# One square per step in the output product, two accumulators apart, and a hinted last branch, in a fused attention and MLP kernel

## The chip, the cores and the metric

The kernel runs on one core of a Trainium2 chip. The metric is the time of one execution on the device, in microseconds (us); lower is better. The names of the engines in the profile are PE (TensorE matmul), PEld (the loading of its weights), DVE (VectorE), ACT (ScalarE), POOL (GpSimd) and SP (SyncE, which issues most transfers). A q behind a name (SPq, ACTq) marks an instruction that the engine's sequencer handles by itself.

## The reference

Attention with a few global columns and a local window over 2 x 768 tokens, 8 heads of 64, is followed by two MLPs on all 1536 tokens.

```python
attn = softmax(scores + bias, masked) @ v            # 2 x 768 tokens, 8 heads of 64
x  = attn.reshape(1536, 512)
xn = x / sqrt(mean(x * x) + 1e-6) * rms_g
g, val = xn @ w_gate, xn @ w_val                     # 512 x 1536 each
y  = (g * sigmoid(g) * val) @ w_out                  # p = g * sigmoid(g) * val; 1536 x 512
h  = relu(y @ w_in)                                  # 512 x 2048
out = (s * h * h + b) @ w_out2                       # 2048 x 512
```

## The kernel before

Weights arrive as float64 words; integer operations on DVE take them apart, and ACT and DVE make of each a high and a low float16 part. Activations are split in the same way, so that each product is three matmuls (`mm3`, L204 to L206: high x high, high x low, low x high). A matmul here is 128 x 128 x 512.

The program for the usual case (`fast_program`) is laid out by hand: each engine works through its own list in order, and waits where an operand isn't ready. After attention, `run` has four products in a row: gate and value (L543), output (L570), in (L622) and the last one (L664). Tokens stand in three blocks of 512 (b = 0, 1, 2).

In the **output product** a step (b, f) has 12 matmuls, three for each m of four accumulators. Ahead of step n+1, `split1(n + 1)` makes the two halves of p: `phi` on ACT (L537) and `plo` on DVE (L538, which reads `phi`). In a step L204 needs `phi`, L205 needs `plo`, and L206 needs `phi` again. The halves have two buffers. `tick` then lets the conversion of a weight advance: L305 and L330 on ACT, L310 to L321 and L335 on DVE.

A float16 program is only right where no value leaves float16's range, so statistics are kept. `see` takes one finished tile of p from the list `unseen` and squares it on ACT with a running sum (`peak`, L511, tile `junk`, and the reading of the sum). In the loop over gate and value one tile is seen after each (f, b); those left over are seen at L568, ahead of the first step of the output product. Near the end `verdict` reduces the statistics to one word, `ok_i`.

In the **last product** block 2 is worked in two passes, over the row tiles t = 0, 1 and t = 2, 3. Its four accumulators are halves of two tiles with two PSUM banks each (`ps("xx")`, t = 0, 1, and `ps("yy")`, t = 2, 3), while block 1 has four tiles of one bank (`ps("gv")`). After the last matmul `evac2` empties t = 2 on DVE (L661) and t = 3 in two halves, one on ACT (L653) and one on DVE (L654), and SP and ACT issue the transfers to `out` (L662, L656, L655).

Then each engine loads `ok_i` (L1218) and branches (L1219): where the word is zero, a general program computes everything again; else the branch leads past it to the end. The bounds given to `values_load` become a check of the word (FUSED_REGOPS and SEQ_ASSERT at L1218), which SP works off behind the second `If`.

Of the kernel before, what the change touches and what calls it, by code (L numbers as in the profile page):

```python
# [29 lines left out]
NB = B * S // BLK  # L30
# [32 lines left out]
def kernel(  # L63
# [17 lines left out]
    nc = tc.nc  # L81
# [70 lines left out]
    ok_i = cst.tile([1, 1], I32, name="ok_i")  # L152
# [9 lines left out]
    def ps(kind):  # L162
        m = banks[kind][turn[kind] % len(banks[kind])]
        turn[kind] += 1
        return psum[0].tile([128, 512] if m < 8 else [128, 2, 512], F32, name=f"ps{m}", tag=f"b{m}")

    def accumulators(second):
        if second:
            return [ps("gv") for _ in range(4)]
        return [t[:, j, :] for t in (ps("xx"), ps("yy")) for j in range(2)]  # L170
# [32 lines left out]
    def mm3(o, ahi, alo, bhi, blo, first, last):  # L203
        T.matmul(out=o, lhsT=ahi, rhs=bhi, start=first, stop=False)  # L204
        T.matmul(out=o, lhsT=ahi, rhs=blo, start=False, stop=False)  # L205
        T.matmul(out=o, lhsT=alo, rhs=bhi, start=False, stop=last)  # L206


    class Mlp:
# [313 lines left out]
        def run(self, done):  # L523
# [9 lines left out]
            def split1(n):  # L533
                b, f = order1[n]
                pt = self.pt.pop((f, b))
                phi, plo = parts[n] = self.split_tiles()
                A.activation(phi, pt, AF.Copy, scale=self.p_scale())  # L537
                V.scalar_tensor_tensor(  # L538
                    plo, in0=pt, scalar=self.p_scale(), in1=self.raw_of(phi), op0=ALU.mult, op1=ALU.subtract
                )  # L540
# [17 lines left out]
            def evac1(acc, yy, m):  # L558
                yhi, ylo = yy
                half = 0.5 * self.up("y") / self.up("p", "w")  # L560
                A.activation(yhi[:, m, :], acc[m], AF.Copy, scale=half)
                V.scalar_tensor_tensor(
                    ylo[:, m, :], in0=acc[m], scalar=half, in1=self.raw_of(yhi[:, m, :]), op0=ALU.mult, op1=ALU.subtract
                )

            self.flush()
            squares = []
            while self.unseen:  # L568
                self.see()
            for n, (b, f) in enumerate(order1):  # L570
                if f == 0:
                    acc = accumulators(b % 2)
                hi, lo = self.get("o", f)
                phi, plo = parts.pop(n)
                for m in range(4):
                    ms = slice(m * 128, (m + 1) * 128)
                    mm3(acc[m], hi[:, ms], lo[:, ms], phi, plo, f == 0, f == F1 - 1)
                if b == NB - 1:
                    self.drop("o", f)
                if n + 1 < len(order1):  # L580
                    split1(n + 1)
                if f == F1 - 1:
                    y[b] = self.new_xy()
                    for m in range(4):
                        self.later(1 + m, lambda acc=acc, b=b, m=m: evac1(acc, y[b], m))
                        squares.append((b, m))
                self.tick(2)
            self.flush()
            p1S.close()
            self.p0S.close()  # L590

# [15 lines left out]
            def split2(n):  # L607
                b, f, t0, t1 = order2[n]
                g = gt[(f, b)] if t1 < 4 else gt.pop((f, b))
                g = g[:, t0 * 128 : t1 * 128]  # L610
                phi, plo = parts[n] = [t[:, : (t1 - t0) * 128] for t in self.split_tiles()]
                A.activation(phi, g, AF.Identity, bias=b_col)  # L612
                V.scalar_tensor_tensor(plo, in0=g, scalar=b_col, in1=self.raw_of(phi), op0=ALU.add, op1=ALU.subtract)  # L613


            order2 = [(b, f, 0, 4) for fs in (range(F2 // 2), range(F2 // 2, F2)) for b in (0, 1) for f in fs]

            order2 += [(b, f, t0, t0 + 2) for b in range(2, NB) for t0 in (0, 2) for f in range(F2)]
            accs = {}
# [21 lines left out]
            with (  # L641
                tc.tile_pool(name="ow", bufs=F2 - RING) as ow,
                tc.tile_pool(name="ob", bufs=4, side="right") as ob,
            ):
                self.xpool["p"] = (ow, lambda f: f >= RING)

                down = 1.0 / self.up("g", "w")

                def evac2(acc, b, t):
                    o = ob.tile([128, BLK], F32, name="o", tag="o")  # L650
                    r0 = self.row_of[4 * b + t]
                    if (b, t) == (NB - 1, 3):
                        A.activation(o[:, HB:], acc[t][:, HB:], AF.Copy, scale=down)  # L653
                        V.tensor_scalar(o[:, :HB], acc[t][:, :HB], down, None, op0=ALU.mult)  # L654
                        nc.scalar.dma_start(out[r0 : r0 + 128, HB:], o[:, HB:])  # L655
                        nc.sync.dma_start(out[r0 : r0 + 128, :HB], o[:, :HB])  # L656
                        return
                    if t % 2:
                        A.activation(o, acc[t], AF.Copy, scale=down)
                    else:  # L660
                        V.tensor_scalar(o, acc[t], down, None, op0=ALU.mult)  # L661
                    nc.sync.dma_start(out[r0 : r0 + 128, :], o)  # L662

                for n, (b, f, t0, t1) in enumerate(order2):  # L664
                    if f == t0 == 0:
                        accs[b] = accumulators(b % 2)
                    acc = accs[b]
                    hi, lo = self.get("p", f)
                    phi, plo = parts.pop(n)
                    for t in range(t0, t1):  # L670
                        ts = slice((t - t0) * 128, (t - t0 + 1) * 128)
                        mm3(acc[t], phi[:, ts], plo[:, ts], hi, lo, f == 0, f == F2 - 1)
                    if n + 1 < len(order2):
                        split2(n + 1)
                    if self.half and n == len(order2) - 24:
                        self.verdict()
                    if f == F2 - 1:
                        for t in range(t0, t1):
                            self.later(1 + (t - t0) // 2, lambda acc=acc, b=b, t=t: evac2(acc, b, t))
                    self.tick(2)  # L680
                self.flush()
# [532 lines left out]
    rv = nc.values_load(fast_i[0:1, 0:1], min_val=0, max_val=1)  # L1214
    with tc.If(rv != 0):
        with tc.manual_schedule(), ExitStack() as fctx:
            fast_program(fctx)
    rv = nc.values_load(ok_i[0:1, 0:1], min_val=0, max_val=1)  # L1218
    with tc.If(rv == 0):  # L1219
        with ExitStack() as gctx:  # L1220
            general_program(gctx)

# [63 lines left out]
```

## Time and profile before

| | us |
|---|---|
| median of 3 runs | 649.4 (648.39 to 649.66) |
| profiled execution, its own time | 648.7 |
| profiled execution, span of the trace | 646.9 |
| PE busy in the span | 624.4 |
| DVE, ACT, POOL busy | 436.3, 310.4, 55.3 |

The span runs from the first to the last instruction on the core; the execution's own time has 1.8 us around it. Times within the trace are counted from the start of the span. Matmuls are pipelined: each is listed with 0.38 us, and in a full stream one starts some 0.22 us after the other.

### The profile page before, as it was taken

How to read it: one execution, taken by the hardware profiler on the slowest of the kernel's cores; microseconds unless marked ns; L12 is line 12 of the kernel's file. 1: busy time of each engine (PE TensorE's matmuls, PEld its weight loads, DVE VectorE, ACT ScalarE, POOL GpSimd, SP SyncE). 2: the span in 40 equal slices, each digit the busy share in tenths (PEclk: the TensorE clock that was granted, in tenths of full speed). 3: DMA queues.
4: the chain of work that ended last, by engine and by line, in shares of the span. 5: the costliest groups of instructions: out<-in, count | busy, mean ns of one | idle time of the engine just before them, and what ended most of it. 6: DMA issues, size and time to landing. Idle time of an engine off the chain costs nothing.

```text
span 646.9 us, 9387 instructions
## 1 busy us (share of the span) xinstructions
PE 624.4 (97%) x3379; PEld 318.8 (49%) x3379; DVE 436.3 (67%) x1103; ACT 310.4 (48%) x689; POOL 55.3 (9%) x59
## 2 busy tenths in 40 slices
PE   9889999999999999997999999999999999999994
PEld 6668777544444444443444444444444444444442
DVE  8898988435888768885342478888666788633452
ACT  4978868413444444465232346644333445333431
POOL 1445552300000000000000000000000000000000
PEclk9999999999999999998999999999999999999998
DMA  8673642001333323332100032333222232010001
GB/s 256 199 217 106 188 141 66 2 2 33 97 98 98 99 73 110 110 97 66 32 1 0 1 97 67 103 108 114 66 66 66 65 99 97 1 65 36 32 33 37
DMA packets 39419, 52.50 MB, mean 81 GB/s; under 512 B 4420, under 2 KB 31300, under 8 KB 39364
## 3 DMA queue, kind: packets, MB, share of 16 engines
q1 hardware_dynamic: 38690, 51.42, 25.4%
q8 instruction: 28, 0.46, 0.3%
q10 hardware_dynamic: 674, 0.39, 0.2%
q14 instruction: 27, 0.22, 0.1%
HBM read 48.66 MB, written 3.15 MB: 80 GB/s over the span
## 4 chain that ended last, share of the span: by engine, by line
PE 88%; DVE 5%; ACT 4%; issue 1%; POOL 1%; DVEq 0%; ACTq 0%; POOLq 0%
PE ps L204 27%; PE ps L206 26%; PE ps L205 26%; PE ps L991 2%; PE ps L972 2%; PE ps L920 2%; ACT t L948 1%; DVE t L933 1%; ACT junk L511 1%; ACT pt L979 1%; PE ps L428 1%; PE ps L441 1%; DVE xn L451 0%; PE ps L178 0%; DVE xyl L466 0%
## 5 line engine op out<-in xcount | busy, mean ns | idle before, releaser
L204 PE MATMUL ps<-hi_p,ev 128*128 128x512 f16 x192 | 72.8, 379 | 0.5 <-ACT ev L612 0.5
L206 PE MATMUL ps<-hi_p,ev 128*128 128x512 f16 x192 | 72.8, 379 | 0.3 <-DVE ev L613 0.3
L613 DVE SCALAR_TENSOR_TENSOR ev<-gt,sbs,ev 128x512 f16<-128x512 f32 (+1 forms) x64 | 39.5, 617 | 49.4 <-ACT ev L612 49.2
L204 PE MATMUL ps<-xyh,hi_i 128*128 128x512 f16 x192 | 72.8, 379 | 0.0
L205 PE MATMUL ps<-xyl,hi_i 128*128 128x512 f16 x192 | 72.8, 379 | 0.0
L206 PE MATMUL ps<-xyh,lo_i 128*128 128x512 f16 x192 | 72.8, 379 | 0.0
L205 PE MATMUL ps<-lo_p,ev 128*128 128x512 f16 x192 | 72.8, 379 | 0.0
L612 ACT ACTIVATE ev<-gt,sbs 128x512 f16<-128x512 f32 (+1 forms) x64 | 39.2, 614 | 66.0 <-PE ps L205 64.4
L204 PE MATMUL ps<-ev,hi_o 128*128 128x512 f16 x144 | 55.1, 382 | 4.7 <-ACT ev L537 4.7
L601 ACT ACTIVATE side<-ps 128x512 f32<-128x512 f32 x48 | 28.7, 597 | 64.2 <-PE ps L206 64.2
L538 DVE SCALAR_TENSOR_TENSOR ev<-p,ev 128x512 f16<-128x512 f32 x36 | 24.9, 692 | 50.1 <-ACT ev L537 50.1
L204 PE MATMUL ps<-xyh,hi_g 128*128 128x512 f16 (+1 forms) x160 | 57.3, 358 | 0.2 <-DVE p L1062 0.2
L204 PE MATMUL ps<-xyh,hi_v 128*128 128x512 f16 (+1 forms) x160 | 57.3, 358 | 0.1
L206 PE MATMUL ps<-xyh,lo_g 128*128 128x512 f16 (+1 forms) x160 | 57.2, 358 | 0.0
L206 PE MATMUL ps<-xyh,lo_v 128*128 128x512 f16 (+1 forms) x160 | 57.2, 358 | 0.0
L205 PE MATMUL ps<-xyl,hi_g 128*128 128x512 f16 (+1 forms) x160 | 57.2, 358 | 0.0
L205 PE MATMUL ps<-xyl,hi_v 128*128 128x512 f16 (+1 forms) x160 | 57.2, 358 | 0.0
L602 DVE SCALAR_TENSOR_TENSOR gt<-side,sbs 128x512 f32<-128x512 f32 x48 | 36.1, 752 | 29.1 <-ACT side L601 29.0
L205 PE MATMUL ps<-ev,hi_o 128*128 128x512 f16 x144 | 55.3, 384 | 0.4 <-DVE ev L538 0.4
L206 PE MATMUL ps<-ev,lo_o 128*128 128x512 f16 x144 | 55.3, 384 | 0.0
L537 ACT ACTIVATE ev<-p 128x512 f16<-128x512 f32 x36 | 22.6, 628 | 56.7 <-PE ps L206 56.7
L948 ACT ACTIVATE t<-t,mn 128x232 f32<-128x232 f32 (+1 forms) x96 | 44.2, 462 | 11.2 <-DVE mn L933 11.1
(152 smaller groups left out, 1080.0 us busy)
## 6 DMA issues: line engine op xcount, KB each, us to landing
raw_i<-in_moe_w_in_dram SPq DMA_DIRECT2D x16, 512.0 KB, 3.6
raw_p<-in_moe_w_out_dram SPq DMA_DIRECT2D x16, 512.0 KB, 3.5
raw_g<-in_moe_w_gate_dram SPq DMA_DIRECT2D x12, 512.0 KB, 3.8
raw_v<-in_moe_w_val_dram SPq DMA_DIRECT2D x12, 512.0 KB, 3.7
raw_o<-in_moe_w_out_dram SPq DMA_DIRECT2D x12, 512.0 KB, 3.5
vw<-in_v_dram SPq DMA_DIRECT2D x10, 512.0 KB, 3.8
q<-in_q_dram SPq DMA_DIRECT2D x11, 256.0 KB, 4.6
out_dram<-o SPq DMA_DIRECT2D x11, 256.0 KB, 2.1
```

Source lines behind the costliest of these rows:

```text
L204: T.matmul(out=o, lhsT=ahi, rhs=bhi, start=first, stop=False)
L205: T.matmul(out=o, lhsT=ahi, rhs=blo, start=False, stop=False)
L206: T.matmul(out=o, lhsT=alo, rhs=bhi, start=False, stop=last)
L537: A.activation(phi, pt, AF.Copy, scale=self.p_scale())
L538: V.scalar_tensor_tensor(plo, in0=pt, scalar=self.p_scale(), in1=self.raw_of(phi), op0=ALU.mult, op1=ALU.subtract)
L601: A.activation(r, o, AF.Relu, scale=1.0 / self.up("y", "w"))
L602: V.scalar_tensor_tensor(g, in0=r, scalar=s_col, in1=r, op0=ALU.mult, op1=ALU.mult, accum_out=self.stat["g"][:, n : n + 1] if self.half el ...
L612: A.activation(phi, g, AF.Identity, bias=b_col)
L613: V.scalar_tensor_tensor(plo, in0=g, scalar=b_col, in1=self.raw_of(phi), op0=ALU.add, op1=ALU.subtract)
L920: T.matmul(out=st["sc", g][:, j, pp, :], lhsT=st["q"][64 * j : 64 * j + 64, pr, :], rhs=st["k"][64 * j : 64 * j + 64, pr, :], start=True, ...
L948: A.activation(t[:, hh, :], t[:, hh, :], AF.Exp, bias=mn[:, hh : hh + 1], scale=-1.0, accum_out=sm[:, hh : hh + 1])
L972: T.transpose(tp[:, m, hh * 128 : (hh + 1) * 128], st["t", g][:, hh, m * kn : (m + 1) * kn], ident)
```

## The change

Four edits. The squares that were left over are no longer taken all at once ahead of the output product: `see` is called in each of its steps, behind `split1(n + 1)`. In the last product, the accumulators t = 2, 3 of block 2 are two `gv` tiles of one bank each. A place is marked at which a hint for the branch labelled "general" is asked for, and that `If` has the label. `values_load` of `ok_i` has no bounds.

```diff
             self.flush()
             squares = []
-            while self.unseen:
-                self.see()
             for n, (b, f) in enumerate(order1):
...
                 if n + 1 < len(order1):
                     split1(n + 1)
+                self.see()
                 if f == F1 - 1:
...
             self.flush()
+            assert not self.unseen
...
                     if f == t0 == 0:
                         accs[b] = accumulators(b % 2)
+                    if f == 0 and t0 == 2 and b == NB - 1:
+                        accs[b][2:] = [ps("gv") for _ in range(2)]
...
                     if self.half and n == len(order2) - 24:
                         self.verdict()
+                    if self.half and n == len(order2) - 2:
+                        tc.mark_branch_hint_location("general", "LikelyTaken")
...
-    rv = nc.values_load(ok_i[0:1, 0:1], min_val=0, max_val=1)
-    with tc.If(rv == 0):
+    rv = nc.values_load(ok_i[0:1, 0:1])
+    with tc.If(rv == 0, label="general"):
```

**ACT's list at the start of the output product.** `junk` is the square of a tile of p, `ev` is `phi`, and `u` and `hi_o` belong to the conversion of a weight. Before:

```order
L511 ACTIVATE junk,stat_p<-p 128x512 x9
L537 ACTIVATE ev_3122<-p 128x512
L305 ACTIVATE u<-raw_o 128x512
L537 ACTIVATE ev_3144<-p 128x512
L330 ACTIVATE hi_o<-u 128x512
L537 ACTIVATE ev_3166<-p 128x512
```

And in the changed kernel, from the same place:

```order
L511 ACTIVATE junk,stat_p<-p 128x512
L537 ACTIVATE ev_3114<-p 128x512
L511 ACTIVATE junk,stat_p<-p 128x512
L305 ACTIVATE u<-raw_o 128x512
L537 ACTIVATE ev_3137<-p 128x512
L511 ACTIVATE junk,stat_p<-p 128x512
L330 ACTIVATE hi_o<-u 128x512
L537 ACTIVATE ev_3160<-p 128x512
```

Nine squares stood ahead of the `phi` of step 1; now one does (the last that the loop over gate and value calls for), and the other eight stand one behind each of the next eight `phi`. DVE's list is the same in this stretch.

**DVE's list, and then ACT's, at the end of the last product** up to the branch on `ok_i`. The names carry their numbers here, and a row ends with what it waits for (PE, DVE, Activation and Pool are the engines, DMAHW the transfers). DVE before:

```order
L661 TENSOR_SCALAR o_5817<-ps9_5462 128x512 [waits DMAHW7_49,PE_49]
L654 TENSOR_SCALAR o_5820<-ps9_5462 128x256 [waits DMAHW4_49,DMAHW0_49,Activation_49]
L1215 UNCONDITIONAL_BRANCH
L1215 UNCONDITIONAL_BRANCH [waits DVE_49]
L1218 TENSOR_LOAD ok_i_107 [waits DVE_49,Pool_49]
```

DVE in the changed kernel:

```order
L661 TENSOR_SCALAR o_5819<-ps2_5647 128x512 [waits DMAHW7_49,PE_49]
L654 TENSOR_SCALAR o_5822<-ps3_5648 128x256 [waits DMAHW4_49,DMAHW0_49,Activation_49]
L1219 UNCONDITIONAL_BRANCH
L1219 UNCONDITIONAL_BRANCH [waits DVE_49]
L1222 TENSOR_LOAD ok_i_107 [waits DVE_49,Pool_49]
```

ACT before:

```order
L653 ACTIVATE o_5820<-ps9_5462 128x256 [waits DMAHW0_49,DVE_49]
L655 DMA out_0_dram<-o_5820 128x256 [waits Activation_49]
L1215 UNCONDITIONAL_BRANCH
L1215 UNCONDITIONAL_BRANCH [waits Activation_49]
L1218 TENSOR_LOAD ok_i_107 [waits DVE_49,Pool_49]
```

ACT in the changed kernel:

```order
L653 ACTIVATE o_5822<-ps3_5648 128x256 [waits DMAHW0_49,PE_49]
L655 DMA out_0_dram<-o_5822 128x256 [waits Activation_49]
L1219 UNCONDITIONAL_BRANCH
L1219 UNCONDITIONAL_BRANCH [waits Activation_49]
L1222 TENSOR_LOAD ok_i_107 [waits DVE_49,Pool_49]
```

L661 now reads another tile than L653 and L654 do, and L653 waits for PE where it waited for DVE; L654 still waits for ACT. No row for a hint stands ahead of the branch.

**The end of SP's list**, behind the transfers of the general program. Before:

```order
L282 DMA raw_o<-in_moe_w_out_dram 128x1024 x12
L276 DMA raw_i<-in_moe_w_in_dram 128x4x256 x16
L282 DMA raw_p<-in_moe_w_out_dram 128x1024 x16
L662 DMA out_dram<-o 128x512 x11
L656 DMA out_dram<-o 128x256
L1219 UNCONDITIONAL_BRANCH x2
L1218 ISA x2
L1281 UNCONDITIONAL_BRANCH
```

And in the changed kernel:

```order
L282 DMA raw_o<-in_moe_w_out_dram 128x1024 x12
L276 DMA raw_i<-in_moe_w_in_dram 128x4x256 x16
L282 DMA raw_p<-in_moe_w_out_dram 128x1024 x16
L662 DMA out_dram<-o 128x512 x11
L656 DMA out_dram<-o 128x256
L1223 UNCONDITIONAL_BRANCH x2
```

The two instructions of the check (ISA x2) and a branch behind them are gone. Apart from the moved squares and what is shown here, the lists of the usual program hold the same rows as before; none of an engine has a row for a hint.

## Rows read from the trace of the kernel before

**Rows 1.** The page, part 1: busy time, share of the span, instructions

```profile
PE 624.4 (97%) x3379; PEld 318.8 (49%) x3379; DVE 436.3 (67%) x1103; ACT 310.4 (48%) x689; POOL 55.3 (9%) x59
```

**Rows 2.** Waits: who waited for whom, us in total, times, longest

```profile
PE ps L204 <- ACT ev L537: 4.7, 1, 4.7
...
PE ps L204 <- ACT ev L612: 0.5, 1, 0.5
```

**Rows 3.** Timeline, start of the output product: start, duration, engine, line

```profile
288.00 0.61 ACT L511 ACTIVATE junk<-p 128x512 bf16<-128x512 f32 x1
...
288.74 0.63 ACT L511 ACTIVATE junk<-p 128x512 bf16<-128x512 f32 x1
...
289.76 0.69 DVE L318 SCALAR_TENSOR_TENSOR u<-raw_o,u 128x512 int32<-128x512 int32 x1
...
290.27 0.38 PE L206 MATMUL ps<-ev,lo_o 128*128 128x512 f16 x1
...
295.28 0.69 DVE L538 SCALAR_TENSOR_TENSOR ev<-p,ev 128x512 f16<-128x512 f32 x1 [4.83 <-ACT ev L537]
...
296.03 0.58 PE L205 MATMUL ps<-ev,hi_o 128*128 128x512 f16 x1 [0.35 <-DVE ev L538]
...
299.37 0.38 PE L204 MATMUL ps<-ev,hi_o 128*128 128x512 f16 x1
```

**Rows 4.** Windows: stretch, length, busy PE, PEld, DVE, ACT, POOL, PEclk, DMA

```profile
295.30:299.40 4.10, 3.75 (x10) 1.26 (x10) 4.07 (x8) 1.66 (x3) 0.00 (x0) 0.58 0.38 111
...
617.20:628.00 10.80, 10.29 (x49) 4.29 (x48) 5.43 (x26) 4.80 (x10) 0.00 (x0) 1.00 0.13 49
...
302.60:305.20 2.60, 2.60 (x14) 1.18 (x13) 1.93 (x6) 1.15 (x2) 0.00 (x0) 1.00 0.59 188
```

**Rows 5.** Timeline of two later steps of the output product

```profile
302.61 0.38 PE L204 MATMUL ps<-ev,hi_o 128*128 128x512 f16 x1
...
302.81 0.63 ACT L537 ACTIVATE ev<-p 128x512 f16<-128x512 f32 x1 [1.33 <-PE ps L206]
303.34 0.61 ACT L330 ACTIVATE hi_o<-u 128x512 f16<-128x512 f32 x1
...
304.08 0.69 DVE L335 SCALAR_TENSOR_TENSOR lo_o<-u,hi_o 128x512 f16<-128x512 f32 x1
...
305.14 0.69 DVE L318 SCALAR_TENSOR_TENSOR u<-raw_o,u 128x512 int32<-128x512 int32 x1
...
305.20 0.38 PE L204 MATMUL ps<-ev,hi_o 128*128 128x512 f16 x1
```

**Rows 6.** Timeline, end of the last product

```profile
637.37 0.38 PE L206 MATMUL ps<-hi_p,ev 128*128 128x512 f16 x1
...
638.01 0.38 PE L206 MATMUL ps<-hi_p,ev 128*128 128x512 f16 x1
638.43 0.69 DVE L661 TENSOR_SCALAR o<-ps 128x512 f32<-128x512 f32 x1 [1.78 <-PE ps L206]
...
639.16 0.38 ACT L653 ACTIVATE o<-ps 128x256 f32<-128x256 f32 x1 [3.02 <-DVE o L661]
...
639.57 0.42 DVE L654 TENSOR_SCALAR o<-ps 128x256 f32<-128x256 f32 x1 [0.45 <-ACT o L653]
640.02 0.33 SPq L656 DMA_DIRECT2D out_dram<-o  x1
```

**Rows 7.** Line 1219: count, ns min/median/max, first and last start us

```profile
L1219 SPq EVENT_SEMAPHORE  x8: 17/17/17, 644.7 to 645.2; - x8
...
L1219 SPq COMPARE_BRANCH  x1: 50/50/50, 641.3 to 641.3; - x1
```

**Rows 8.** Line 1218, the check on SP

```profile
L1218 SPq FUSED_REGOPS  x1: 164/164/164, 645.3 to 645.3; - x1
L1218 SPq SEQ_ASSERT  x1: 29/29/29, 645.5 to 645.5; - x1
```

**Rows 9.** Transfers: line, KB each, us from issue to landing

```profile
out_dram<-o SPq DMA_DIRECT2D x1, 128.0 KB, 2.1
```

## The prediction

> **What bounds the kernel now.** I read the page first: PE is busy for 624.4 of 646.9 us [rows 1], so time can only go where PE stands still, where its clock is low, or behind its last matmul. The waits tell where it stands still longest: once, 4.7 us, L204 for `phi` (ACT, L537) [rows 2]. The timeline puts this at step 1 of the output product [rows 3]: the last matmul of step 0 starts at 290.27, and ACT works off nine squares, the first at 288.00, one every 0.74 us, before it makes the `phi` that step 1 needs. PE takes up L205 at 296.03, and its starts come in their usual distance again only from 299.37. That distance is 0.216 us: twelve starts from 302.61 to 305.20 [rows 5]. [...] The second place is the end: from the last matmul at 638.01 to the end of the span, 8.9 us. There three evacuations run one behind the other, each waiting for the one before [rows 6], then the last transfer is issued, and SP passes its branch at 641.3 and goes on at 644.7 [rows 7].
>
> **The change part by part.** The sum is made against the profiled execution (648.7 us, span 646.9). The median of the three runs, 649.4, lies 0.7 above it, and I subtract the sum from the median.
>
> **Squares, what is removed.** From 290.27 to 299.37 ten matmuls start, which take 10 x 0.216 = 2.16 us in a full stream; 9.10 passed. So the pile of squares costs 6.94 us: some 5.3 of waiting, and 3.34 - 8 x 0.216 = 1.61 of low clock between 296.03 and 299.37 [rows 3].
>
> **Squares, what is left of the stall.** One square still stands ahead of the `phi` of step 1, so `phi` starts at 288.74, where the second square started, and ends before the step could start at 290.27 + 0.22 = 290.49: L204 doesn't wait. But `plo` (L538) stands behind L318 in DVE's list, which starts at 289.76 and takes 0.69; `plo` then starts at 290.45 at the latest. L205 came 0.75 after the start of `plo` (295.28 to 296.03), so it comes at 291.20 and not at 290.70: 0.50 us stay lost [rows 3]. The bounds are 0 (DVE starts instructions a little before the one ahead has ended) and 0.50 + 1.61 = 2.11, if the clock falls in spite of so short a wait. I take 0.50, since from 617.2 to 628 the clock stayed at 1.00 [rows 4] although PE stood still there for 0.5 us [rows 2]. The gain is 6.94 - 0.50 = 6.44, between 4.83 and 6.94.
>
> **Squares, where they go.** Eight of them now stand in steps 1 to 8, behind the `phi` of the next step, 0.74 us each. I cost them at nothing; the work that covers them is PE's, 2.59 us a step. ACT in a step: 0.53 from `phi` to the next start, 0.74 for the square, 0.61 for L330, or 1.88 [rows 5, 3]. What comes late is the weight conversion: L330 starts at 303.34 + 0.74 and ends 0.61 later, 304.69, so DVE's L335 starts 0.6 later than at 304.08, and with it L318, from 305.74 to 306.43 [rows 5]. Behind it in DVE's list is the `plo` of the step that starts at 305.20 + 2.59 = 307.79; it could start at 306.43 and let L205 go at 307.18, which is due at 308.0: 0.8 us to spare. The weight parts that are delayed are needed only some steps later. Were the cover gone, each square would cost up to 0.74, all eight 5.9.
>
> **Accumulators apart.** With t = 2 and t = 3 in tiles of their own, L661 waits only for the last matmul of t = 2. That one starts at 637.37, 0.64 before the last of all, and an evacuation starts 0.42 after such a start (638.01 to 638.43): L661 runs from 637.79 to 638.48, beside PE. L653 waits for PE instead of DVE, so it starts at 638.43 and not at 639.16. L654 still waits for L653: 0.41 later, at 638.84 instead of 639.57. The last transfer is issued 0.73 us earlier [rows 6]. Whether the end follows: the transfer lands 2.1 us after its issue [rows 9], at 642.1 as it is now, and SP comes to its waits at 644.7 [rows 7]; the landing is not what SP waits for, so everything behind moves with the issue. Gain 0.73, with 0 as the lower bound if another engine came last, and 1.07 as the upper, if L654 no longer stayed behind L653 (638.50 instead of 639.57).
>
> [...]
>
> **The check.** SP runs it between its waits and its end: 164 and 29 ns [rows 8]. SP's eight waits of 17 ns take 0.5 us [rows 7], so an instruction costs some 0.05 beyond its duration: 0.19 + 2 x 0.05 = 0.3 us, an estimate between 0.19 and 0.4. SP is alone there, and the end waits for it.
>
> **The hint.** The changed lists have no row for it on any engine, so I cost it at 0; the 3.3 us between SP's branch and its next instruction [rows 7] stay.
>
> **Sum:** 6.44 + 0.73 + 0.3 = 7.5 us. The profiled execution would take 641.2, the median 641.9.
>
> **The rivals.**
>
> *The hint works (chance 0.04).* If the branch did know its target ahead, SP would go on at 641.4 and wait for the landing at 642.1 in its sixth wait, which it now passes at about 645.05: 2.9 us less, 639.0. For it: DVE, ACT and SP each have a branch there, and SP's 3.3 us are a wait for nothing that the program computes. Against: the lists show nothing that would tell the sequencer. [...]
>
> *The clock still falls (0.08).* The wait that is left, 0.50 us or a little more, lets the clock fall as before: 1.61 us come back, 643.5. Against it is the stretch from 617.2.
>
> *The squares only move (0.04).* Each step waits for its square after all, 0.74 x 8 = 5.9 us: 647.8, faster by a quarter per cent. The spare 0.8 us would have to be wrong by as much.
>
> *Slower (0.03).* [...]
>
> *The squares move without cost and the stall stays (0.01).* Something else than the squares holds `phi` of step 1; no row names it. Then 648.4.
>
> **How the numbers follow.** My forecast, 7.5 us less, has 0.80. Its own range is from the bounds: 4.83 to 6.94, 0.19 to 0.4 and 0 to 1.07 are not all at one end together, so some 6.5 to 8.3, or 641.1 to 642.9. The three runs lie 1.0 below to 0.3 above their median, and the case with the low clock is at 643.5; the range 640.2 to 643.9 takes in both, and leaves out the working hint and the three dear cases, 0.12 with some noise beyond. A measurement of this kernel can tell about 0.2% (1.3 us) from no change. Faster by more: my forecast, the hint, the low clock, and half of the case in which the squares only move, 0.94; within 0.2%: 0.03; slower: 0.03.
>
> **What would show each step.** In the waits, L204 for `phi` of L537 goes from 4.7 us to nearly nothing and L205 for `plo` stays below 0.6; the clock has no stretch below 1.00 between 290 and 300; in the timeline one square stands in each step behind `phi`, and starts of PE in steps 1 to 8 come every 0.216 us. L653 starts with the last matmul's end and no longer after L661, and line 1222 has no FUSED_REGOPS on SP, while SP's branch is still followed by some 3.3 us. I would be wrong if PE waited for `plo` in each step, if the clock fell, if another engine came to the end later than SP, or if SP's gap had shrunk.

## The result and the profile after

| | before | after |
|---|---|---|
| median of 4 runs each, us | 648.89 (647.92 to 649.66) | 641.01 (640.72 to 643.17) |
| ratio, 95% interval | | 0.9886 (0.986 to 0.9913) |
| profiled execution: its time, its span | 648.7, 646.9 | 643.2, 641.4 |

By the medians the change makes the kernel 7.9 us faster, by the means of the four runs 7.4; 7.5 were forecast. The ratio is estimated from all runs, so here and below it needn't be that of the two medians. The profiled execution of after is the slowest of its four; why comes below, with the clock.

The waits of PE, after (who waited for whom, us in total, times, longest). The 4.7 us of L204 for `phi` [rows 2] have no row any more, and what took their place is 0.2:

```profile
PE ps L204 <- ACT ev L612: 0.5, 1, 0.5
...
PE ps L206 <- DVE ev L613: 0.3, 1, 0.3
...
PE ps L205 <- DVE ev L538: 0.2, 1, 0.2
```

The timeline at the start of the output product, after, in the columns of [rows 3]:

```profile
289.89 0.38 PE L204 MATMUL ps<-ev,hi_o 128*128 128x512 f16 x1
...
289.99 0.61 ACT L511 ACTIVATE junk<-p 128x512 bf16<-128x512 f32 x1
...
290.60 0.61 ACT L537 ACTIVATE ev<-p 128x512 f16<-128x512 f32 x1
...
291.12 0.61 ACT L511 ACTIVATE junk<-p 128x512 bf16<-128x512 f32 x1
...
291.75 0.69 DVE L318 SCALAR_TENSOR_TENSOR u<-raw_o,u 128x512 int32<-128x512 int32 x1
...
292.26 0.38 PE L206 MATMUL ps<-ev,lo_o 128*128 128x512 f16 x1
...
292.36 0.68 DVE L538 SCALAR_TENSOR_TENSOR ev<-p,ev 128x512 f16<-128x512 f32 x1
292.48 0.38 PE L204 MATMUL ps<-ev,hi_o 128*128 128x512 f16 x1
...
293.10 0.38 PE L205 MATMUL ps<-ev,hi_o 128*128 128x512 f16 x1 [0.24 <-DVE ev L538]
...
293.31 0.38 PE L206 MATMUL ps<-ev,lo_o 128*128 128x512 f16 x1
```

One square stands ahead of the `phi` of step 1 and one behind it. L204 starts 0.22 behind the last matmul of step 0, without a wait; L205 starts 0.62 behind L204 instead of 0.216, since `plo` stood behind L318 on DVE (291.75 to 292.44; `plo` started at 292.36): 0.40 us are left of the stall. From there the starts come every 0.216 us. From the last matmul of step 0 (292.26) to the last of the kernel (633.46, below) 341.20 us pass; before it was 290.27 to 638.01 [rows 3, 6], or 347.74. So 6.54 us came from here.

The windows, after, in the columns of [rows 4]. There is no low clock at the output product, but an early stretch at half the clock:

```profile
20.90:27.80 6.90, 6.58 (x35) 4.31 (x33) 6.57 (x30) 5.14 (x17) 3.29 (x2) 0.51 0.62 204
290.50:295.30 4.80, 4.56 (x22) 2.00 (x21) 4.77 (x10) 3.67 (x10) 0.00 (x0) 1.00 0.37 118
295.30:299.40 4.10, 4.10 (x21) 1.86 (x20) 3.47 (x8) 2.94 (x7) 0.00 (x0) 1.00 0.42 130
```

The end of the last product, after, answers to [rows 6]:

```profile
633.23 0.69 DVE L661 TENSOR_SCALAR o<-ps 128x512 f32<-128x512 f32 x1 [1.13 <-PE ps L206]
...
633.46 0.38 PE L206 MATMUL ps<-hi_p,ev 128*128 128x512 f16 x1
633.88 0.38 ACT L653 ACTIVATE o<-ps 128x256 f32<-128x256 f32 x1 [2.30 <-PE ps L206]
...
634.29 0.42 DVE L654 TENSOR_SCALAR o<-ps 128x256 f32<-128x256 f32 x1 [0.37 <-ACT o L653]
634.75 0.99 SPq L656 DMA_DIRECT2D out_dram<-o  x1
```

L661 runs beside PE, L653 waits for PE and no longer for L661, and L656 is issued 1.29 behind the last matmul's start instead of 2.01. But the issue takes 0.99 us instead of 0.33. SP's branch and what follows it, after [rows 7]:

```profile
L1223 SPq EVENT_SEMAPHORE  x8: 17/17/17, 639.5 to 640.0; - x8
...
L1223 SPq COMPARE_BRANCH  x1: 50/50/50, 636.7 to 636.7; - x1
```

The gap is 2.8 us, where it was 3.4; line 1222 has no FUSED_REGOPS and no SEQ_ASSERT [rows 8]. From the last matmul's start to the end of the span 7.93 us pass (641.39 - 633.46) instead of 8.90: 0.97 us came from the end. With 6.54 that is 7.5, as in the sum.

### The profile page after: what moved, and what is told of

Read it like the earlier page. It is cut to its first block, busy times and chain, and to the rows that moved or that the text cites. A ratio compares the mean times of both kernels' runs of the same rounds, so it can differ in the third digit from the quotient of the medians.

```text
span 641.4 us, 9381 instructions
## 1 busy us (share of the span) xinstructions
PE 624.7 (97%) x3379; PEld 319.6 (50%) x3379; DVE 435.9 (68%) x1103; ACT 309.4 (48%) x689; POOL 55.4 (9%) x59
## 4 chain that ended last, share of the span: by engine, by line
PE 90%; DVE 5%; ACT 2%; POOL 1%; issue 1%; DVEq 0%; ACTq 0%; POOLq 0%
PE ps L204 27%; PE ps L206 27%; PE ps L205 27%; PE ps L995 3%; PE ps L924 3%; PE ps L976 3%; DVE t L937 1%; ACT t L952 1%; PE ps L428 1%; PE ps L178 1%; ACT pt L983 1%; PE ps L441 1%; DVE xn L451 0%; DVE xyl L466 0%; DVE p L1066 0%
## 5 line engine op out<-in xcount | busy, mean ns | idle before, releaser
L204 PE MATMUL ps<-hi_p,ev 128*128 128x512 f16 x192 | 72.8, 379 | 0.5 <-ACT ev L612 0.5
L204 PE MATMUL ps<-xyh,hi_i 128*128 128x512 f16 x192 | 72.8, 379 | 0.0
L205 PE MATMUL ps<-xyl,hi_i 128*128 128x512 f16 x192 | 72.8, 379 | 0.0
L205 PE MATMUL ps<-lo_p,ev 128*128 128x512 f16 x192 | 72.8, 379 | 0.0
L601 ACT ACTIVATE side<-ps 128x512 f32<-128x512 f32 x48 | 28.7, 597 | 64.1 <-PE ps L206 64.1
L204 PE MATMUL ps<-xyh,hi_g 128*128 128x512 f16 (+1 forms) x160 | 57.3, 358 | 0.2 <-DVE p L1066 0.2
L204 PE MATMUL ps<-xyh,hi_v 128*128 128x512 f16 (+1 forms) x160 | 57.3, 358 | 0.1
L205 PE MATMUL ps<-xyl,hi_g 128*128 128x512 f16 (+1 forms) x160 | 57.2, 358 | 0.0
L205 PE MATMUL ps<-xyl,hi_v 128*128 128x512 f16 (+1 forms) x160 | 57.2, 358 | 0.0
L205 PE MATMUL ps<-ev,hi_o 128*128 128x512 f16 x144 | 54.6, 379 | 0.2 <-DVE ev L538 0.2
L204 PE MATMUL ps<-ev,hi_o 128*128 128x512 f16 x144 | 54.6, 379 | 0.0
L488 ACT ACTIVATE side<-ps 128x512 f32<-128x512 f32 x28 | 16.7, 597 | 65.3 <-PE ps L206 65.3
```

The lines of the kernel that those rows point to most:

```text
L601: A.activation(r, o, AF.Relu, scale=1.0 / self.up("y", "w"))
```

## The experiments

Each profiled execution can be cut at the same three places, read from its timeline: when the first matmul of the output product starts; how long from there to the start of the last matmul of all (**D1**); and how long from that to the end of the span (**D2**). The three add up to the span. The column behind the start says how long, in the first 30 us, the granted clock stood at half.

| kernel | first start | clock at half early | D1 | D2 |
|---|---|---|---|---|
| before | 287.90 | 0 | 350.12 | 8.90 |
| after | 289.89 | 6.83 | 343.57 | 7.93 |
| e1_squares | 287.69 | 0 | 343.58 | 8.92 |
| e2_accs | 287.69 | 0 | 349.74 | 7.77 |
| e3_check | 289.33 | 3.41 | 351.23 | 8.70 |
| e4_hint_all | 287.95 | 0 | 343.58 | 5.52 |
| e5_two | 287.79 | 0 | 343.58 | 7.72 |
| e6_three | 288.70 | 3.41 | 346.01 | 7.84 |
| e7_pile3 | 290.03 | 6.83 | 344.75 | 7.66 |
| e8_pile5 | 287.80 | 0 | 346.23 | 7.66 |
| e9_hint_early_late | 290.03 | 6.83 | 343.26 | 5.54 |
| e10_best | 287.80 | 0 | 343.26 | 5.63 |
| e11_hint_sp | 287.89 | 0 | 343.57 | 6.09 |
| e12_hint_before | 290.06 | 6.83 | 349.70 | 6.25 |

The first start tells why runs of the kernel after lie up to 2.5 us apart: an early stretch at half the granted clock (0.51 from 20.90 to 27.80 in after) comes in some executions, with the change and without it, and the first start is then 0.9 to 2.3 us later. D1 and D2 don't hold it, so they compare kernels better than single times do; D1 of the four kernels with the changed squares and no other work there agrees within 0.01. D1 of the four with the whole pile doesn't (349.70 to 351.23). Behind the wait, matmuls start late as long as the clock stands at half (0.50 for 3.41 us in before, below): six in e2 and e12, eight in before and thirteen in e3, at a cost of 1.2, 1.2, 1.6 and 2.7 us. A row of the table is one profiled execution; each time below is set against the kernel before as it ran beside it (648.55, 649.64 or 648.60 us).

**The parts, each alone on the kernel before.**

```diff
# e1_squares
-            while self.unseen:
-                self.see()
...
                     split1(n + 1)
+                self.see()
```

> The kernel before with the squares of p taken one per step, and nothing else of the change. My sum gives 6.44 us less than before (6.94 for the pile, 0.50 left at L205): from a median of 648.9 to 642.5, a ratio of 0.990. In the trace no wait of L204 for phi of step 1, a granted clock of 1.00 from 290 to 300 us, and 8.9 us from the start of the last matmul to the end of the span, as before. Rival one: only the waiting goes and the clock falls all the same, 4.8 us less, 644.1. Rival two: the whole measured difference of 7.9 us comes from the squares and the end brings nothing, 641.0.

Measured: 642.19 against 648.55, ratio 0.9904 (0.9884 to 0.9923): 6.4 us. D1 is 6.54 shorter and D2 the same. The waits of PE have the same 0.2 at L205 as after, and the windows of e1_squares, in the columns of [rows 4], show a clock of 1.00:

```profile
290.00:300.00 10.00, 9.76 (x47) 4.32 (x45) 8.90 (x18) 6.78 (x16) 0.00 (x0) 1.00 0.35 110
```

Both rivals fall: the clock's share came back too, and the end brings something of its own.

```diff
# e2_accs
                         accs[b] = accumulators(b % 2)
+                    if f == 0 and t0 == 2 and b == NB - 1:
+                        accs[b][2:] = [ps("gv") for _ in range(2)]
```

> The kernel before with the last two accumulators apart, and nothing else of the change. My sum gives 0.73 us less: from 648.9 to 648.2, and from the start of the last matmul to the end of the span 8.2 us instead of 8.9; L653 starts with the last matmul's end and no longer behind L661, and the last transfer is issued 0.73 us earlier. Rival: what stands behind SP's branch sets the end by itself, the distance stays at 8.9 us and the time at 648.9, though L653 comes earlier.

Measured: 648.01 against 648.55, ratio 0.9992 (0.9979 to 1.0006), which says no more than that it is small. D2 says more: 7.77 instead of 8.90, 1.13 less. The timeline of e2_accs at its end:

```profile
637.43 0.38 PE L206 MATMUL ps<-hi_p,ev 128*128 128x512 f16 x1
637.84 0.38 ACT L653 ACTIVATE o<-ps 128x256 f32<-128x256 f32 x1 [2.30 <-PE ps L206]
...
638.71 0.53 SPq L656 DMA_DIRECT2D out_dram<-o  x1
```

SP's branch and its waits behind it, line 1221 of e2_accs:

```profile
L1221 SPq EVENT_SEMAPHORE  x8: 17/17/17, 643.0 to 643.5; - x8
...
L1221 SPq COMPARE_BRANCH  x1: 50/50/50, 640.2 to 640.2; - x1
```

L656 is issued 1.28 behind the last matmul's start instead of 2.01, the 0.73 of the sum. The issue takes 0.20 longer, and the gap behind the branch is 0.6 shorter (640.2 to 643.0, against 641.3 to 644.7): -0.73 + 0.20 - 0.6 = -1.13. Why the gap shrank the runs don't settle: it is 3.4 us where L661 holds L653 back (before, e1, e3), and 2.6 to 2.8 in the six kernels without a hint where it doesn't, the kernel after among them. Set against e3 (D2 8.70), which has the check out and the accumulators together, the five kernels with both parts and no hint (after, e5 to e8) have 7.66 to 7.93: there the accumulators bring 0.8 to 1.0.

```diff
# e3_check
-    rv = nc.values_load(ok_i[0:1, 0:1], min_val=0, max_val=1)
+    rv = nc.values_load(ok_i[0:1, 0:1])
```

> The kernel before without the bounds on the value that is loaded for the last branch, and nothing else of the change. My sum gives 0.3 us less (0.19 to 0.4): the median falls from 648.9 to 648.6, less than a comparison of medians can tell; in the trace FUSED_REGOPS and SEQ_ASSERT are gone from line 1222's place on SP, and from the start of the last matmul to the end of the span 8.6 us pass instead of 8.9. Rival: SP's gap behind the branch grows by as much, and the distance stays at 8.9 us.

Measured: 649.2 against 648.55, ratio 1.0002 (0.9988 to 1.0015): nothing that a time can tell. D2 is 8.70 instead of 8.90. Line 1218 has a TENSOR_LOAD on SP and nothing behind it; SP's branch is at 643.9 and its first wait at 647.3, a gap as before. So 0.2, the lower end of the term.

**The hint.** In the change it names no engine, and no list has a row for it. With engines named there is one row per engine:

```diff
# e4_hint_all
-                        tc.mark_branch_hint_location("general", "LikelyTaken")
+                        tc.mark_branch_hint_location("general", "LikelyTaken", engines=mybir.ALL_ENGINES)
```

> The changed kernel with the hint given for all engines, so that each engine's list holds one hint row; it stands at the start of the fast block, some 600 us ahead of the branch that it is for. My theory, that a hint this far ahead covers nothing: 641.0 us as the changed kernel, and SP still stands 2.8 to 3.4 us between its branch and its next instruction. Rival, that the hint was only missing in the list: SP goes on 2.5 to 3 us earlier and waits for the last transfer's landing, some 638.4 us.

Measured: 638.87 against 641.01 of the changed kernel (ratio to before 0.986, 0.9839 to 0.9882). My theory falls. The hint stands on SP at 4.2 us, and at 634.6 SP's branch is followed by its next instruction after 0.5 us instead of 2.8; PE's branch itself takes 383 ns instead of 3819. The hint's row on SP in e4_hint_all:

```profile
L1285 SPq BRANCH_PREFETCH_HINT  x1: 56/56/56, 4.2 to 4.2; - x1
```

The branch, line 1223 of e4_hint_all:

```profile
L1223 SPq EVENT_SEMAPHORE  x8: 17/17/17, 635.1 to 635.6; - x8
...
L1223 PEldq COMPARE_BRANCH  x1: 383/383/383, 631.1 to 631.1; - x1
...
L1223 SPq COMPARE_BRANCH  x1: 70/70/70, 634.6 to 634.6; - x1
```

The two queues that the profile lists as instruction, after (packets, MB, share of 16 engines):

```profile
q8 instruction: 28, 0.46, 0.3%
...
q14 instruction: 27, 0.22, 0.1%
```

The same in e4_hint_all:

```profile
q8 instruction: 27, 0.44, 0.3%
...
q14 instruction: 24, 0.20, 0.1%
```

D2 falls by 2.41, to 5.52, and four transfers of instructions fewer run. By their times in the trace all four are missing behind the last matmul, where 8 run in the kernel after and 4 in e4 (e12 below has 4 there too, before 8); ahead of it both kernels have the same number. So with a hint that ran 630 us earlier the gap behind SP's branch is 0.5 us instead of 2.8. That the gap was a wait for instructions is my reading of these counts, and no run shows it by itself; how the hint covers it is not shown either: no additional transfer stands ahead of the branch.

```diff
# e11_hint_sp: as e4_hint_all, but
+                        tc.mark_branch_hint_location("general", "LikelyTaken", engines=[mybir.EngineType.SP])
```

> The changed kernel with the hint for SP alone. If the gap behind SP's branch is what the end waits for, SP goes on 0.5 us behind its branch and the other engines come next, ACT at some 5.1 us behind the start of the last matmul: from that start to the end of the span 5.7 to 6.1 us instead of 7.7, and 639.1 to 639.5. Rival: the gap needs every engine's hint, or ACT's and DVE's gaps hold the end by themselves: 641.0.

Measured: 639.54 (ratio to before 0.9864, 0.9846 to 0.9883), D2 6.09. SP alone brings 1.8 of the 2.4 us; then ACT and DVE, whose branches still have their gaps (3.1 us each, from 633.6 to 636.7 on ACT and from 633.3 to 636.4 on DVE), come last. One transfer of instructions is missing here, where the hint for all engines took away four (q8 has 28 as after). The other queue in e11_hint_sp:

```profile
q14 instruction: 26, 0.21, 0.1%
```

Line 1223 of e11_hint_sp:

```profile
L1223 SPq COMPARE_BRANCH  x1: 70/70/70, 634.7 to 634.7; - x1
...
L1223 DVEq EVENT_SEMAPHORE  x1: 21/21/21, 636.4 to 636.4; - x1
L1223 ACTq EVENT_SEMAPHORE  x1: 17/17/17, 636.7 to 636.7; - x1
```

```diff
# e12_hint_before: the kernel before, and
+                    if self.half and n == len(order2) - 2:
+                        tc.mark_branch_hint_location("general", "LikelyTaken", engines=mybir.ALL_ENGINES)
...
-    with tc.If(rv == 0):
+    with tc.If(rv == 0, label="general"):
```

> The kernel before with the hint for all engines and nothing else of the change. If the hint's gain stands by itself, 2.4 us less: from the start of the last matmul to the end of the span 6.5 us instead of 8.9, and 646.5 against 648.9, a ratio of 0.9963. Rival: it needs the earlier evacuations too (SP then meets the wait for the last transfer's landing, which comes 0.73 us later here), and 1.7 us or less are gained, 647.2.

Measured: 646.96 against 648.6, ratio 0.9961 (0.9946 to 0.9976), D2 6.25 instead of 8.90. By the ratio that is 2.5 us (the medians lie 1.6 apart), by D2 2.65: the hint's gain stands by itself and is of the expected size.

**Whether the eight squares are free in the steps.**

```diff
# e5_two (e6_three: again * 2)
                     split1(n + 1)
+                again = self.unseen[:1]
                 self.see()
+                for f2, b2, pt in again * 1:
+                    self.peak("p", NB * f2 + b2, pt, self.p_scale())
```

> The changed kernel with each of the eight squares of the output product's steps taken twice, one behind the other, into the same place of the statistics (the additional squares are not part of the reference). My theory, that they lie in idle time of ACT and DVE: ACT then has 0.54 + 2 x 0.61 to 0.74 + 0.61, or 2.4 to 2.6 us, in a step of 2.59, and the plo of DVE comes up to 0.74 later of the 0.8 that it has to spare, so no more than 0.3 us are lost: 641.0 to 641.3. Rival, that the cover is gone already and each further square costs its time: 8 x 0.74 more, 646.9.

Measured: 640.97 (ratio to before 0.9878), and D1 343.58, as after to a hundredth. Eight squares more cost nothing. What they used up of the spare time is seen at the step that starts 13.35 behind the first, whose `plo` stands behind a conversion. The timeline there, after:

```profile
301.12 0.69 DVE L318 SCALAR_TENSOR_TENSOR u<-raw_o,u 128x512 int32<-128x512 int32 x1
...
301.73 0.68 DVE L538 SCALAR_TENSOR_TENSOR ev<-p,ev 128x512 f16<-128x512 f32 x1
...
303.45 0.38 PE L205 MATMUL ps<-ev,hi_o 128*128 128x512 f16 x1
```

The same step in e5_two:

```profile
299.78 0.69 DVE L318 SCALAR_TENSOR_TENSOR u<-raw_o,u 128x512 int32<-128x512 int32 x1
...
300.39 0.68 DVE L538 SCALAR_TENSOR_TENSOR ev<-p,ev 128x512 f16<-128x512 f32 x1
...
301.36 0.38 PE L205 MATMUL ps<-ev,hi_o 128*128 128x512 f16 x1
```

Where L205 waited for `plo`, it came some 0.74 behind its start (292.36 to 293.10 above). After, it comes 1.72 behind it here, so 1.0 us is to spare; with two squares 0.97, and 0.2 is left.

> The changed kernel with each of those eight squares taken three times (sixteen squares more than the reference needs). My theory: now the cover is too short. ACT has 3.0 to 3.4 us of work in a step of 2.59 and falls behind by 0.4 to 0.8 a step; phi was some 2 us early at first, so 1 to 4 us are lost over eight steps, and DVE's plo, later by 1.2 to 1.5 us with 0.8 to spare, waits in the steps with a conversion: 642.5 to 645. Rival, that squares are hidden at any number: 641.0. Rival, that each costs its time: 16 x 0.74 more, 652.8.

Measured: 643.86 (ratio 0.9914, 0.9889 to 0.9938), D1 346.01, 2.43 more than after. The waits of PE in e6_three:

```profile
PE ps L205 <- DVE ev L538: 2.4, 3, 1.1
```

It is DVE's `plo` behind the conversion that comes late, by 1.2 us in each of two steps, and not ACT's `phi`: no wait of L204 for L537 shows. So of the theory's two terms the one for `plo` came and the one for `phi` did not, and the time lies in its range; the rivals are off by 3 and 9 us.

**How much pile does what.**

```diff
# e7_pile3 (e8_pile5: range(5))
             squares = []
+            for _ in range(3):
+                self.see()
             for n, (b, f) in enumerate(order1):
```

> The changed kernel with three of the squares put back ahead of the output product, five still one per step. By the times of the kernel before, phi of step 1 ends 3 x 0.74 later than without a pile, so L204 waits 1.1 us and L205 is 1.6 us late in all, 1.2 more than in the changed kernel. If only a longer wait lets the granted clock fall, 642.2 and a clock of 1.00; if waits of a microsecond let it fall, 1.6 more, 643.8, with a stretch at 0.5 behind the wait.

Measured: 643.65 (642.02 to 644.21; ratio 0.9901, 0.9879 to 0.9922). The median would suit the low clock, but D1 is 344.75, 1.18 more than after, and the granted clock behind the wait is 1.00; what lifts the time is the early stretch, 6.83 us in the profiled execution. So it was the first of the two theories: a wait of 0.90 us (L204 for `phi`, 1.28 us between two starts of PE) cost itself and no more here.

> The changed kernel with five of the squares put back ahead of the output product, three one per step. phi of step 1 ends 5 x 0.74 later than without a pile, L204 waits 2.6 us and L205 is 3.1 us late in all, 2.7 more than in the changed kernel: 643.7 if the clock stays at 1.00, 645.3 if it falls as it did in the kernel before. I expect the fall here, and that wait and clock together are the 6.9 us that the whole pile cost.

Measured: 643.41 (ratio 0.9913, 0.9891 to 0.9935), D1 346.23, 2.66 more than after. The wait is of the expected size, but the clock doesn't fall. The timeline of e8_pile5:

```profile
290.17 0.38 PE L206 MATMUL ps<-ev,lo_o 128*128 128x512 f16 x1
...
292.94 0.38 PE L204 MATMUL ps<-ev,hi_o 128*128 128x512 f16 x1 [2.39 <-ACT ev L537]
...
293.67 0.38 PE L205 MATMUL ps<-ev,hi_o 128*128 128x512 f16 x1 [0.35 <-DVE ev L538]
```

The windows of e8_pile5, in the columns of [rows 4]:

```profile
290.00:300.00 10.00, 7.26 (x34) 3.14 (x33) 6.89 (x14) 8.59 (x22) 0.00 (x0) 1.00 0.20 61
```

Two starts 2.77 us apart left the granted clock at 1.00; three of the four times of e8, this execution's among them, lie within 0.2 us of each other, so it was no single case. In the kernel before the starts are 5.03 apart, and the clock went to half, for 3.41 us in before, e2 and e12 and for 6.83 in e3, whose D1 is 1.1 to 1.5 longer for it. The expectation that five squares bring the fall was wrong. The window of before, in the same columns:

```profile
295.92:299.33 3.41, 3.30 (x8) 1.13 (x8) 3.38 (x8) 1.04 (x2) 0.00 (x0) 0.50 0.44 128
```

**Towards a faster kernel.** What was left in the profile after: 0.40 at L205, and late starts behind evacuations in the last product.

```diff
# e9_hint_early_late: e4_hint_all, and
                         split1(0)
+                        split1(1)
...
-                if n + 1 < len(order1):
+                if 0 < n < len(order1) - 1:
                     split1(n + 1)
...
-                            self.later(1 + (t - t0) // 2, lambda acc=acc, b=b, t=t: evac2(acc, b, t))
+                            self.later(2 + (t - t0) // 2, lambda acc=acc, b=b, t=t: evac2(acc, b, t))
```

> The changed kernel with the hint for all engines, with phi and plo of step 1 made right behind those of step 0 (ahead of the conversion that held plo), and with the evacuations of a finished pass given out one step later, behind the parts of the next step but one. From the kernel with the hint for all engines, 638.9: 0.40 less at L205 of step 1, and 0.49 and 0.67 less at the two starts in the last product that come late behind evacuations (at some 510 and 612 us): 637.3, and no start of PE more than 0.3 us behind the one before it in either product. Rival: what is put back behind the evacuations comes late in its turn, or the conversion that now stands behind plo holds a later step, and the time stays at 638.9.

Measured: 638.85 against 638.87 with the hint alone (ratio to before 0.9848, 0.9831 to 0.9865). D1 is 0.32 shorter: the 0.40 at L205 are gone, no start in the output product is late, and the later evacuations lose 0.08. The timeline of e9_hint_early_late shows why; its lines stand one behind those of after:

```profile
613.24 0.69 DVE L662 TENSOR_SCALAR o<-ps 128x512 f32<-128x512 f32 x1
...
614.00 0.60 ACT L660 ACTIVATE o<-ps 128x512 f32<-128x512 f32 x1 [1.81 <-DVE o L662]
...
614.50 0.90 ACT L613 ACTIVATE ev<-gt,sbs 128x256 f16<-128x256 f32 x2
...
615.05 0.39 PE L204 MATMUL ps<-hi_p,ev 128*128 128x512 f16 x1 [0.60 <-ACT ev L613]
```

ACT's evacuation of t = 1 waits for DVE's of t = 0, as L653 waited for L661 before the change: the two lie in one tile. Until then ACT holds the `phi` that PE needs next, one step later than it did. The rival had it right. Taking t = 0 and 1 apart too, as the change does with 2 and 3, wasn't tried.

```diff
# e10_best: e9_hint_early_late, and
-                        A.activation(o[:, HB:], acc[t][:, HB:], AF.Copy, scale=down)
-                        V.tensor_scalar(o[:, :HB], acc[t][:, :HB], down, None, op0=ALU.mult)
-                        nc.scalar.dma_start(out[r0 : r0 + 128, HB:], o[:, HB:])
-                        nc.sync.dma_start(out[r0 : r0 + 128, :HB], o[:, :HB])
+                        A.activation(o, acc[t], AF.Copy, scale=down)
+                        nc.scalar.dma_start(out[r0 : r0 + 128, :], o)
```

> The same, and the last 128 rows evacuated whole by ACT (0.60 us, as L659 takes) and sent from ACT's queue in one transfer, in place of two halves on two engines one behind the other and two transfers. The last transfer is then issued about 1.05 us behind the start of the last matmul instead of 1.28, in one issue instead of two; from that start to the end of the span 5.1 to 5.4 us instead of 5.52, and the time 636.9 to 637.2. Rival: the one transfer is twice as large and lands later by 0.3 us or more, SP waits for it, and nothing is gained or 0.3 lost: 637.3 to 637.6.

Measured: 638.69 (638.59 to 640.45; ratio 0.9854, 0.9836 to 0.9872), D2 5.63. The rival again. The last transfer's issue in the timeline of e10_best:

```profile
632.10 0.39 ACTq L655 DMA_DIRECT2D out_dram<-o  x1
```

The same transfer with its size and its time from issue to landing:

```profile
out_dram<-o ACTq DMA_DIRECT2D x1, 256.0 KB, 3.0
```

SP's waits behind its branch, line 1222 of e10_best:

```profile
L1222 SPq EVENT_SEMAPHORE  x8: 17/17/17, 633.5 to 635.3; - x8
```

SP is at its waits at 633.5 and stands in them until the transfer has landed, 632.1 + 3.0 = 635.1. So in e10 the landing sets the end. In e4 it doesn't: SP passes its eight waits there in the same 0.5 us as before (635.1 to 635.6 above). e4, e9 and e10 can't be told apart by their times; each is some 2.2 us faster than the kernel after.

## Why the prediction was right

**Squares, 6.44 forecast.** D1 fell by 6.55, and e1 alone by 6.4 us of time. The working holds in each piece: in the profiled execution of before the pile cost 5.3 of waiting and 1.6 of low clock, and all of it came back but 0.40 at L205 behind L318, forecast as 0.50. The agreement to 0.1 holds for the one execution of before from which the sum was worked out: the low clock cost 1.2 to 2.7 us in the four executions with the pile, and against D1 of e2 or e3 the same squares gain 6.2 or 7.7. The choice that mattered was that so short a wait leaves the clock alone; e7 and e8 show that even 1.3 and 2.8 us between starts do (1.00 in both, where before had 0.50 for 3.41 us behind 5.03). The rival *the clock still falls* is out.

**Squares in the steps, 0.** Shown by e5 and e6: two per step cost nothing, three cost 2.43 us, on the chain that the prediction named (conversion on ACT, conversion on DVE, `plo`). The spare time was 1.0 us instead of 0.8. The prediction's "steps 1 to 8" should read steps 0 to 7 (the first of the eight squares starts at 291.12, before step 1 does at 292.48), which leaves its sum as it is. With that *the squares only move* and *slower* are out: no run shows the clock at half through all eight steps, and in after it was 1.00 from 289.89 to 311.00.

**Accumulators apart, 0.73.** The move of the last issue is right to a hundredth, but the step "everything behind moves with the issue" is not: the issue takes 0.2 to 0.7 us longer, and SP's gap is 0.6 us shorter, which the prediction had named as a sign of being wrong. Why either changed stays open. Alone the part brings 1.13, above the upper bound of 1.07; beside the other parts 0.8 to 1.0. That L653 waits for L661 no longer once the two read tiles of their own is borne out: it came earlier by the 0.73 (0.42 behind the last matmul's start instead of 1.15), and e9 shows the wait once more where t = 0 and 1 lie in one tile (ACT's evacuation at 614.00, behind DVE's from 613.24).

**The check, 0.3.** 0.20 in e3, at the low end of 0.19 to 0.4: the 0.05 us that the sum added for each of the two instructions do not show.

**The hint, 0.** Right for the change as it stands, and for the reason given: no list has a row for it. What the prediction said in the rival *the hint works* was right in its place (SP's wait behind the branch) and near in size, 2.9 us against 2.4 of D2 and 2.1 of time, once the hint names its engines.

The errors at the end cancel by luck in the profiled execution: 0.97 us against 0.73 + 0.3. The 0.4 us between the forecast and the medians' difference is less than what the early stretch of low clock moves single runs by.

## What to carry to other kernels

Work that ACT had gathered ahead of a new stage cost there nearly its whole length (5.3 of 8 x 0.74 us), and the low clock after it (1.6 us) where the wait was long: the clock fell where 5.03 us passed between two starts, and held where 2.77 did. Spread over the steps it was free up to the spare time of the chain that it delayed, which the rows gave (1.0 us a step, one square more but not two). Two engines that evacuated halves of one tile ran one after the other (L653 0.73 us behind the start of L661, and 0.76 between the two starts in e9): look for an evacuation that waits for another engine's. The hint counted only once it had a row in the engines' lists: look for the row of a hint, a flag or an option; here a missing argument was worth 2.1 us.

## What the runs showed of the hardware

- A branch hint that ran 630 us ahead of its branch cut the gap behind it from 2.8 to 0.5 us on SP, and PE's branch from 3819 to 383 ns (e4). One transfer of instructions behind the branch went with the hint for SP alone (e11), four with that for all engines (e4, e12).
- The issue of L656 took 0.33 us behind L661 and L653 in a row, and 0.53 to 1.01 where the accumulators lie apart (0.53 in e2, 0.99 after, 1.01 in e5); its transfer landed 2.3 to 3.6 us after its start (3.2 after) instead of 1.9 to 2.1 [rows 9]. The cause was not looked into.
- The granted clock stayed at 1.00 over 2.77 us without a start of PE (e8) and fell to half where 5.03 passed without one (before). In the attention stage it fell at some 20 to 21 us, for 3.41 or 6.83 us, in six of the fourteen profiled executions; what sets it off there stays open.
